# Attention times values in whole float32, two heads in one bank, in a fused attention and two-layer-stack kernel

## The chip, the cores and the metric

The kernel runs on one core of one Trainium2 chip, as one launch. The metric is the device time of that launch in microseconds, the median of several executions. The core's engines are TensorE (PE in the profile; PEld is its loading of stationary operands), VectorE (DVE), ScalarE (ACT), GpSimd (POOL) and SyncE (SP), which here only issues transfers. Each engine works through its own instructions in the order of the program and waits for others by semaphores.

## What is computed

Inputs are whole float32. Three stages follow each other: causal attention with a decay, a maximum of three projections, and a rational function between two projections.

```python
scores = q @ k.T / 8                      # (4, 8, 576, 576), head_dim 64
decay  = cum[:, :, :, None] - cum[:, :, None, :]      # cum = cumsum(log(clip(f)))
scores = where(causal, -1e9, scores + decay)
attn   = softmax(scores)                  # with 1e-9 in the denominator
x = (attn @ v)                            # -> (2304, 512)
h = maximum(maximum(x @ w1, x @ w2), x @ w3)          # d_ff 768
x2 = h @ w_out                            # (2304, 512)
g = P(x2 @ w_in) / (Q(x2 @ w_in) + 1e-6)  # d_ff 2048, P cubic, Q quadratic
out = g @ w_out2
```

## The kernel before

The eight heads of a batch are taken as four **pairs**, two heads side by side in 128 partitions or columns. The 576 queries form two **groups** `g`: queries 0 to 319 (g 0, three blocks) and 320 to 575 (g 1, two blocks). A **unit** is one head and one group of a pair. The loop over `slots` takes one unit a step: in step s the unit's scores are made and exponentiated (`scores`, L348 on), in step s+1 its probabilities are turned (`turn`, L392 on: TensorE transposes into `tp`, copies into `pt`), in step s+2 they are multiplied with the values (`attend`, L427 on). Batch 0 has eight pairs of one group each; the other three batches have twelve pairs of both groups. There are 32 products of a pair and a group in all, each for two heads.

**Two ways of a product.** TensorE multiplies either whole float32 (`F32`) or a shorter format (`F32R`). Pairs 0 to 5 (`WHOLE`) use whole float32: `turn` copies `tp` once (L418), `attend` multiplies with 64 columns of values (L437), and each head's result lies in `ot[0:64]`. The other 14 pairs (2 with g 1 alone, 12 with both groups: 26 pair-groups, 52 units) use two F32R parts. ACT copies the high part (L420), DVE subtracts the low part (L423); POOL splits the values likewise (`split_v`, L312 and L313); the stationary operand holds 64 columns of high and 64 of low values, and the product (L449) streams the high and the low probabilities through all 128 columns: 9 matmuls for g 1, 5 for g 0. The two halves of `ot` are then added (L460 on ACT, L461 on DVE), and POOL splits the sum into two F32R parts for the next stage (L464, L465).

**Beside it** the planner `fill`, called six times a step, spreads three kinds of other work over the steps: the first layer of the next stage for batches whose attention is done (`moe1_h` L489 to L496, `moe1_o` L513 to L518), the conversion of weights (`convert`, L162 to L172: `cv_w`, `cv_wo`, and from step 32 `cv_wp`), and the preparation of the next pair's keys and queries. A scheduler orders each engine's instructions from this program; it may move them across steps. For the first four pairs `exercised` puts two matmuls on a constant (L81) ahead of each new bank. The bank pool `ps_o` of the product has one buffer.

After the loop the weights of the last stage are converted (`cv_wi`), and the last stage (L736 to L796) runs on TensorE, untouched by the change.

Of the kernel before, what the change touches and what calls it, by code (L numbers as in the profile page):

```python
# [34 lines left out]
def kernel(  # L35
# [60 lines left out]
    ones = apool.tile([NR, S], F32, name="ones", tag="e4")  # L96
# [34 lines left out]
    vn = apool.tile([P, NB, 2, D], F32, name="vn")  # L131
# [7 lines left out]
    ptfs = {}  # L139
# [94 lines left out]
    class Pair:  # L234


        def __init__(self, n, b, hp, groups):
# [5 lines left out]
            self.x32, self.vs = {}, {}  # L243
# [10 lines left out]
        def load_v(self):  # L254
            b, h0 = self.b, 2 * self.hp
            if self.whole:
                self.v = apool.tile([P, NB, 2, D], F32, name=f"v_{self.n}", tag="vs", bufs=3)
                load_nat(self.v, v, b, h0, 0, self.nk)
                return
            load_nat(vn, v, b, h0, 0, self.nk)  # L260
            nc.sync.dma_start(vn[D:P, 0], v[b, h0 : h0 + 2, 0:D].rearrange("h p d -> p h d"))
# [61 lines left out]
    class Unit:  # L323


        def __init__(self, pair, h, g):
            self.pair, self.h, self.g, self.nm = pair, h, g, f"{pair.n}_{h}_{g}"
            self.e = {}

            self.alt = pair.b == 0 and h == 1  # L330

        def begin(self):
            if self.alt:
                name = f"ea_{self.nm}"
                if self.g == 0:
                    ea = [apool.tile([P, 576], F32, name=name + "2", tag="e4")]
                    ea.append(apool.tile([P, 448], F32, name=name + "1", tag="e3"))
                    self.e = {2: ea[0][:, :320], 1: ea[1][:, :192], 0: ea[1][:, 192:256]}
                else:
                    ea = apool.tile([P, 2 * GCOLS[0]], F32, name=name, tag="pt0")  # L340
                    self.e = {4: ea[:, :576], 3: ea[:, 576:1024]}
# [5 lines left out]
        def scores(self, i):  # L347
# [6 lines left out]
            if not self.alt:  # L354
                self.e[i] = apool.tile([P, keys], F32, name=f"e{i}_{self.nm}", tag=f"e{i}")
# [33 lines left out]
        def turn(self, bank):  # L389

            g = self.g
            hi = GQ[g][1]  # L392
            if self.pair.whole:
                if g not in ptfs:
                    ptfs[g] = apool.tile([P, 2, GCOLS[g]], F32, name=f"ptf{g}", tag=f"pt{g}")
                self.pt = ptfs[g][:, self.h]
            elif bank == 0:
                tag = f"pt{1 if self.alt else g}"
                self.pt = apool.tile([P, 2, GCOLS[g]], F32R, name=f"pt_{self.nm}", tag=tag)
            pt = self.pt  # L400
# [16 lines left out]
            if self.pair.whole:  # L417
                nc.scalar.activation(pt[:kr, base : base + n], tp[:kr, :n], AF.Copy)  # L418
                return
            nc.scalar.activation(pt[:kr, 0, base : base + n], tp[:kr, :n], AF.Copy)  # L420

            lo = pt[D:P, 0] if chunks[0] == 0 else pt[:, 1]
            nc.vector.tensor_tensor(  # L423
                lo[:kr, base : base + n], tp[:kr, :n], r32(pt[:kr, 0, base : base + n]), op=ALU.subtract
            )

        def attend(self):  # L427
            p, h, g = self.pair, self.h, self.g
            lo, hi = GQ[g]
# [3 lines left out]
            a, o = SIDES[h]  # L433
            if p.whole:
                for j, (c, (col, q0)) in enumerate(order):
                    kr = Q1[c] - Q0[c]
                    nc.tensor.matmul(  # L437
                        ot[0:D, q0 - lo : w], p.v[:kr, c, h], self.pt[:kr, col : col + hi - q0],
                        start=(j == 0), stop=(j == len(order) - 1),
                    )  # L440
                if h == 0:
                    xt[p.b, p.hp, g] = mpool.tile([P, 2, w], F32R, name=f"x_{self.nm}", tag=f"x{g}", bufs=(6, 8)[g])
                x = xt[p.b, p.hp, g]
                nc.scalar.activation(x[a, 0], ot[0:D, :w], AF.Copy)
                nc.vector.tensor_tensor(x[a, 1], ot[0:D, :w], r32(x[a, 0]), op=ALU.subtract)
                return
            for j, (c, (col, q0)) in enumerate(order):
                for s in range(1 if c == 0 else 2):
                    nc.tensor.matmul(  # L449
                        ot[:, q0 - lo : w],  # L450
                        p.vs[h][:, c].rearrange("p t d -> p (t d)"),
                        self.pt[:, s, col : col + hi - q0],
                        start=(j == 0 and s == 0),
# [138 lines left out]
    for p in pairs:  # L592
# [4 lines left out]
        if p.n:  # L597
            lvat.setdefault(max(0, at - LV), []).append(p)
# [264 lines left out]
```

## Time and profile before

| | us |
|---|---|
| median of 3 runs (lowest, highest) | 1027.72 (1026.54, 1028.21) |
| the profiled execution | 1026.19 |
| its span, first to last instruction | 1024.4 |
| PE, DVE, ACT, POOL busy | 977.5, 845.5, 624.6, 358.3 |

The profiled execution takes 1.8 us more than its span. A matmul's recorded time includes the way through the array, and the next starts before it ends; so what a matmul costs is read from the start of it to the start of the next, and a PE that is shown as busy may still hold gaps. In a row of the timeline the first number is the start, the second the time from the first start to the last end, both in us, and x9 counts the instructions merged. A row of groups has the source line, engine, operation, output and inputs, shape and count, then the busy time in us and the mean of one in ns, then the engine's idle time ahead of it and who ended that. A row of stretches has the stretch, its length, and for PE, PEld, DVE, ACT and POOL the busy time in us with the number of instructions, then the share of full clock that TensorE was granted, the transfers' share and their GB/s. The line of a chain gives the shares of a stretch that lines had in the chain of work that ended last.

### The profile page before, as it was taken

How to read it: one execution, taken by the hardware profiler on the slowest of the kernel's cores; microseconds unless marked ns; L12 is line 12 of the kernel's file. 1: busy time of each engine (PE TensorE's matmuls, PEld its weight loads, DVE VectorE, ACT ScalarE, POOL GpSimd, SP SyncE). 2: the span in 40 equal slices, each digit the busy share in tenths (PEclk: the TensorE clock that was granted, in tenths of full speed). 3: DMA queues.
4: the chain of work that ended last, by engine and by line, in shares of the span. 5: the costliest groups of instructions: out<-in, count | busy, mean ns of one | idle time of the engine just before them, and what ended most of it. 6: DMA issues, size and time to landing. Idle time of an engine off the chain costs nothing.

```text
span 1024.4 us, 17331 instructions
## 1 busy us (share of the span) xinstructions
PE 977.5 (95%) x5736; PEld 852.7 (83%) x5736; DVE 845.5 (83%) x1908; ACT 624.6 (61%) x1441; POOL 358.3 (35%) x606
## 2 busy tenths in 40 slices
PE   8989889998899999999999889999999999999998
PEld 5657777996888888899999788888888888899997
DVE  4779998778888988975759785998988888799997
ACT  4675656557555555554544335866666766677775
POOL 1536766666566666664636450000000000000000
PEclk9999999998899998999999999999999999999999
DMA  4664223123234434512034628501101100200000
GB/s 124 167 169 136 75 52 102 31 57 107 76 108 132 150 110 147 168 48 77 9 103 125 196 83 288 205 1 42 42 0 62 42 1 1 81 23 1 31 1 31
DMA packets 120472, 87.16 MB, mean 85 GB/s; under 512 B 69296, under 2 KB 105152, under 8 KB 120384
## 3 DMA queue, kind: packets, MB, share of 16 engines
q1 hardware_dynamic: 120384, 86.08, 27.6%
q8 instruction: 45, 0.74, 0.3%
q14 instruction: 43, 0.35, 0.1%
HBM read 63.36 MB, written 22.69 MB: 84 GB/s over the span
## 4 chain that ended last, share of the span: by engine, by line
PE 64%; DVE 20%; issue 5%; ACT 4%; POOL 3%; DMA 3%; SPq 1%; POOLq 0%; DVEq 0%; ACTq 0%
PE oo L786 6%; PE oo L787 6%; PE oo L785 6%; PE hq L736 6%; PE hq L738 6%; PE hq L737 6%; PE tp L413 4%; PE h L489 3%; PE h L490 3%; PE h L491 3%; PE o L449 2%; DVE e L371 2%; DVE pt L423 2%; DVE cv_wp L163 2%; DVE m L496 1%
## 5 line engine op out<-in xcount | busy, mean ns | idle before, releaser
L489 PE MATMUL h<-x,w1h 128*128 128x320 f32 (+1 forms) x576 | 176.1, 306 | 5.9 <-DVE m L496 3.6
L490 PE MATMUL h<-x,w1h 128*128 128x320 f32 (+1 forms) x576 | 172.2, 299 | 0.0
L491 PE MATMUL h<-x,w1l 128*128 128x320 f32 (+1 forms) x576 | 171.3, 298 | 0.0
L489 PEld LDWEIGHTS h<-x,w1h 128*128 128x128 f32 x576 | 109.6, 190 | 10.4 <-DVE m L496 5.4
L786 PE MATMUL oo<-wp,gh 128*128 128x512 f32 x288 | 112.8, 392 | 0.0
L785 PE MATMUL oo<-wp,gh 128*128 128x512 f32 x288 | 112.4, 390 | 0.0
L377 ACT ACTIVATE e<-e,st 64x64 f32<-64x64 f32 (+4 forms) x140 | 78.2, 559 | 52.8 <-DVE st L371 50.1
L490 PEld LDWEIGHTS h<-x,w1h 128*128 128x128 f32 x576 | 109.8, 191 | 0.4 <-issue 0.2
L491 PEld LDWEIGHTS h<-x,w1l 128*128 128x128 f32 x576 | 109.5, 190 | 0.1
L787 PE MATMUL oo<-wp,gl 128*128 128x512 f32 x288 | 108.8, 392 | 0.0
L745 ACT ACTIVATE s<-hq 128x512 f32<-128x512 f32 (+1 forms) x80 | 44.3, 554 | 97.2 <-PE hq L738 97.1
L387 POOL TENSOR_SCALAR e<-e,rs 64x64 f32<-64x64 f32 (+4 forms) x140 | 76.8, 560 | 62.1 <-DVE rs L383 46.4
L748 DVE SCALAR_TENSOR_TENSOR s<-s,ab,u 128x512 f32<-128x512 f32 (+1 forms) x80 | 55.9, 698 | 30.9 <-ACT u L746 30.7
L423 DVE TENSOR_TENSOR pt<-tp,pt 128x384 fp32r<-128x384 f32 (+3 forms) x132 | 69.9, 539 | 10.2 <-ACT pt L420 7.8
L371 DVE CUSTOM_DVE_ANT_0 e<-s,mask 128x320 f32<-128x320 f32 (+3 forms) x140 | 58.8, 431 | 22.7 <-PE s L367 9.0
L413 PE MATMUL tp<-ident,e 128*128 128x128 f32 (+2 forms) x420 | 70.8, 283 | 2.9 <-POOL e L387 1.4
L420 ACT ACTIVATE pt<-tp 128x384 fp32r<-128x384 f32 (+3 forms) x132 | 57.7, 473 | 24.5 <-PE tp L413 23.4
L738 PE MATMUL hq<-x,wil 128*128 128x512 f32 (+1 forms) x192 | 70.4, 366 | 0.0
L736 PE MATMUL hq<-x,wih 128*128 128x512 f32 (+1 forms) x192 | 70.4, 366 | 0.0
L737 PE MATMUL hq<-x,wih 128*128 128x512 f32 (+1 forms) x192 | 70.3, 366 | 0.0
L513 PE MATMUL x2p<-hh,wo 128*128 128x320 f32 (+1 forms) x192 | 58.5, 307 | 9.6 <-POOL hh L500 7.9
L787 PEld LDWEIGHTS oo<-wp,gl 128*128 128x128 f32 x288 | 54.1, 188 | 11.6
(145 smaller groups left out, 2718.9 us busy)
## 6 DMA issues: line engine op xcount, KB each, us to landing
raw_w<-in_moe_w_dram SPq DMA_DIRECT2D x18, 512.0 KB
raw_wp<-in_moe_w_out_dram SPq DMA_DIRECT2D x32, 256.0 KB
wpd<-wp SPq DMA_DIRECT2D x32, 256.0 KB
raw_wi<-in_moe_w_in_dram SPq DMA_DIRECT2D x32, 256.0 KB
wp<-wpd SPq DMA_DIRECT2D x10, 768.0 KB
x2d<-xo SPq DMA_DIRECT2D x16, 320.0 KB
out_dram<-ob SPq DMA_DIRECT2D x18, 256.0 KB
kn<-in_k_dram SPq DMA_DIRECT2D x32, 128.0 KB
```

The source lines that it names most:

```text
L371: nc.vector.tensor_tensor_reduce(out=e[:nr, a:z], in0=sp[:nr, : z - a], in1=mask[:nr, off + a : off + z], scale=-1.0, scalar=3.0e38 if n = ...
L413: nc.tensor.transpose(tp[:kr, dst : dst + nr], self.e[i][:nr, Q0[c] : Q1[c]], ident[:nr, :nr])
L423: nc.vector.tensor_tensor(lo[:kr, base : base + n], tp[:kr, :n], r32(pt[:kr, 0, base : base + n]), op=ALU.subtract)
L489: nc.tensor.matmul(hp_[:, :w], wh[:, j, dc], xs[dc][:, 1], start=(dc == NDC - 1), stop=False)
L490: nc.tensor.matmul(hp_[:, :w], wh[:, j, dc], xs[dc][:, 0], start=False, stop=False)
L491: nc.tensor.matmul(hp_[:, :w], wl[:, j, dc], xs[dc][:, 0], start=False, stop=(dc == 0))
L736: nc.tensor.matmul(hp_[:, :w], wih[:, dc, fs], xh, start=(dc == 0), stop=False)
L737: nc.tensor.matmul(hp_[:, :w], wih[:, dc, fs], xl, start=False, stop=False)
L738: nc.tensor.matmul(hp_[:, :w], wil[:, dc, fs], xh, start=False, stop=(dc == NDC - 1))
L785: nc.tensor.matmul(o, g[0][:, ts_], wh_, start=(fc == 0), stop=False)
L786: nc.tensor.matmul(o, g[0][:, ts_], wl_, start=False, stop=False)
L787: nc.tensor.matmul(o, g[1][:, ts_], wh_, start=False, stop=(fc == NF2 - 1))
```

## The change

Every product of probabilities and values is made in whole float32. `split_v`, the low part of `pt`, the sum of halves and the split on POOL are gone; values are loaded straight into one of three buffers `vs`. A product waits until both heads of a pair and group are turned; it is issued once for both, alternating between them, head 0 into `ot[0:64]` and head 1 into `ot[64:128]` (`SIDES`), each with a stationary operand of 64 columns. The result is copied by ACT and its rest subtracted by DVE, both on 128 partitions. Units of a pair are ordered group 0 head 0, group 0 head 1, group 1 head 0, group 1 head 1, where it was head by head. The score tiles `e` have a buffer for each head, so the borrowed tiles (`alt`) of batch 0 go.

```diff
         def load_v(self):
             b, h0 = self.b, 2 * self.hp
-            if self.whole:
-                self.v = apool.tile([P, NB, 2, D], F32, name=f"v_{self.n}", tag="vs", bufs=3)
-                load_nat(self.v, v, b, h0, 0, self.nk)
-                return
-            load_nat(vn, v, b, h0, 0, self.nk)
-            nc.sync.dma_start(vn[D:P, 0], v[b, h0 : h0 + 2, 0:D].rearrange("h p d -> p h d"))
+            self.v = apool.tile([P, NB, 2, D], F32, name=f"v_{self.n}", tag="vs", bufs=3)
+            load_nat(self.v, v, b, h0, 0, self.nk)
...
-        def split_v(self, h):
-            if self.whole:
-                return
-            nk = self.nk
-            vs = apool.tile([P, NB, 2, D], F32R, name=f"vs{h}_{self.n}", tag="vs", bufs=3)
-            pinned(nc.gpsimd.tensor_scalar(vs[:, :nk, h], vn[:, :nk, h], 1.0, 0.0, op0=ALU.mult, op1=ALU.add))
-            nc.gpsimd.tensor_tensor(vs[:, :nk, 1 - h], vn[:, :nk, h], r32(vs[:, :nk, h]), op=ALU.subtract)
-            self.vs[h] = vs
...
-            if not self.alt:
-                self.e[i] = apool.tile([P, keys], F32, name=f"e{i}_{self.nm}", tag=f"e{i}")
+            self.e[i] = apool.tile([P, keys], F32, name=f"e{i}_{self.nm}", tag=f"e{i}_{h}")
...
-            if self.pair.whole:
-                nc.scalar.activation(pt[:kr, base : base + n], tp[:kr, :n], AF.Copy)
+            nc.scalar.activation(pt[:kr, base : base + n], tp[:kr, :n], AF.Copy)
+
+        def attend(self):
+
+            p, h, g = self.pair, self.h, self.g
+            if h == 0:
                 return
-            nc.scalar.activation(pt[:kr, 0, base : base + n], tp[:kr, :n], AF.Copy)
-
-            lo = pt[D:P, 0] if chunks[0] == 0 else pt[:, 1]
-            nc.vector.tensor_tensor(
-                lo[:kr, base : base + n], tp[:kr, :n], r32(pt[:kr, 0, base : base + n]), op=ALU.subtract
-            )
...
-            if p.whole:
-                for j, (c, (col, q0)) in enumerate(order):
-                    kr = Q1[c] - Q0[c]
+            for j, (c, (col, q0)) in enumerate(order):
+                kr = Q1[c] - Q0[c]
+                for i in range(2):
                     nc.tensor.matmul(
-                        ot[0:D, q0 - lo : w], p.v[:kr, c, h], self.pt[:kr, col : col + hi - q0],
+                        ot[SIDES[i][0], q0 - lo : w], p.v[:kr, c, i], p.pt[g][:kr, i, col : col + hi - q0],
                         start=(j == 0), stop=(j == len(order) - 1),
                     )
...
-            half = apool.tile([P, 320], F32, name=f"half_{self.nm}", tag="half")[:, :w]
-            nc.scalar.activation(half[a], ot[o, :w], AF.Copy)
-            nc.vector.tensor_tensor(x32[a], ot[a, :w], half[a], op=ALU.add)
-            if h == 1:
-                x = mpool.tile([P, 2, w], F32R, name=f"x_{self.nm}", tag=f"x{g}", bufs=(6, 8)[g])
-                nc.gpsimd.tensor_scalar(x[:, 0], x32, 1.0, 0.0, op0=ALU.mult, op1=ALU.add)
-                nc.gpsimd.tensor_tensor(x[:, 1], x32, r32(x[:, 0]), op=ALU.subtract)
-                xt[p.b, p.hp, g] = x
+            x = mpool.tile([P, 2, w], F32R, name=f"x_{self.nm}", tag=f"x{g}", bufs=(6, 8)[g])
+            nc.scalar.activation(x[:, 0], ot[:, :w], AF.Copy)
+            nc.vector.tensor_tensor(x[:, 1], ot[:, :w], r32(x[:, 0]), op=ALU.subtract)
+            xt[p.b, p.hp, g] = x
...
-    slots = [Unit(p, h, g) for p in pairs for h in range(2) for g in p.groups]
+    slots = [Unit(p, h, g) for p in pairs for g in p.groups for h in range(2)]
```

On PE the product of head 1 and g 1 of pair 17 (`o`, from the turned `pt` and the split values `vs`) stands like this before, amid the second projection of the first layer (`x2p`) and the next pair's scores (`s`):

```order
L514 MATMUL x2p_0_3_6588<-hh_0_4_6262,wo_1445 128x320
L449 MATMUL o_1_1_6572<-pt_1_1_6478,vs_17_6346 128x256 x7
L449 MATMUL o_1_1_6572<-pt_1_1_6478,vs_17_6346 128x128 x2
L515 MATMUL x2p_0_3_6588<-hh_0_4_6262,wo_1445 128x320
L513 MATMUL x2p_0_3_6588<-hh_0_5_6422,wo_1542 128x320
L514 MATMUL x2p_0_3_6588<-hh_0_5_6422,wo_1542 128x320
L515 MATMUL x2p_0_3_6588<-hh_0_5_6422,wo_1542 128x320
L369 MATMUL s_0_18_0_1_6642<-k1s_1112,q1s_1175 128x448
```

One head's nine matmuls stand together, on 128 output partitions; head 0's nine stand at another place. For the same pair and group the changed program has, with the product now at L399 and `v` unsplit:

```order
L455 MATMUL x2p_0_2_6010<-hh_0_5_5907,wo_1499 128x320
L399 MATMUL o_1_1_6038<-pt_0_1_5853,v_5518 64x256
L453 MATMUL x2p_0_3_6052<-hh_0_0_5268,wo_1075 128x320
L454 MATMUL x2p_0_3_6052<-hh_0_0_5268,wo_1075 128x320
L455 MATMUL x2p_0_3_6052<-hh_0_0_5268,wo_1075 128x320
L453 MATMUL x2p_0_3_6052<-hh_0_1_5423,wo_1175 128x320
L454 MATMUL x2p_0_3_6052<-hh_0_1_5423,wo_1175 128x320
L455 MATMUL x2p_0_3_6052<-hh_0_1_5423,wo_1175 128x320
L453 MATMUL x2p_0_3_6052<-hh_0_2_5543,wo_1252 128x320
L454 MATMUL x2p_0_3_6052<-hh_0_2_5543,wo_1252 128x320
L455 MATMUL x2p_0_3_6052<-hh_0_2_5543,wo_1252 128x320
L399 MATMUL o_1_1_6038<-pt_0_1_5853,v_5518 64x256 x7
```

Both heads' products stand together, on 64 output partitions each, and the first one (head 0, keys 0 to 63) was moved ahead of nine other matmuls, alone. It stands apart in 29 of the 32 products.

On DVE, in the stretch where the scheduler works on pairs 13 and 14, the program before has the low parts of `pt` between the conversion of weights (`cv_wp`) and the masking of scores (L371, printed as ISA):

```order
L168 SCALAR_TENSOR_TENSOR cv_wp_0_4485<-raw_wp_0_4311,cv_wp_0_4485 128x256
L423 TENSOR_TENSOR pt_1_1_4425<-tp_13_1_1_4426,pt_1_1_4425 128x512
L165 SCALAR_TENSOR_TENSOR cv_wp_1_4572<-raw_wp_1_4370,cv_wp_1_4572 128x256
L371 ISA e_14_0_1_4604,st_0_1_4602<-s_0_14_0_1_4605,mask 128x448
L371 ISA st_0_1_4602 128x1
L518 TENSOR_TENSOR xo_0_2_4452<-x2p_0_2_4433,xo_0_2_4452 128x320
L371 ISA e_14_0_1_4628,st_0_1_4602<-s_0_14_0_1_4629,mask 128x320
L371 ISA st_0_1_4602 128x1
L423 TENSOR_TENSOR pt_1_1_4425<-tp_13_1_1_4456,pt_1_1_4425 128x384
L423 TENSOR_TENSOR pt_1_1_4425<-tp_13_1_1_4462,pt_1_1_4425 64x256
```

The changed program, near the end of pair 13's attention, has there (masking is now L344):

```order
L344 ISA e_14_1_0_4251,st_1_0_4248<-s_0_14_1_0_4252,mask 64x64
L344 ISA st_1_0_4248 64x1
L355 TENSOR_SCALAR rs_0_0_4121<-rs_0_0_4121 128x3
L356 RECIPROCAL rs_0_0_4121<-rs_0_0_4121 128x3
L458 TENSOR_TENSOR xo_0_3_4166<-x2p_0_3_4147,xo_0_3_4166 128x320
L161 TENSOR_SCALAR cv_wp_0_4290<-cv_wp_0_4290 128x256
L162 TENSOR_SCALAR cv_wp_0_4290<-cv_wp_0_4290 128x256
L163 SCALAR_TENSOR_TENSOR cv_wp_0_4290<-raw_wp_0_4135,cv_wp_0_4290 128x256
L166 SCALAR_TENSOR_TENSOR cv_wp_0_4290<-raw_wp_0_4135,cv_wp_0_4290 128x256
L405 TENSOR_TENSOR x_1_1_4207<-o_1_1_4196,x_1_1_4207 128x256
```

The low parts are gone; one subtraction for a pair and group (L405) stands in place of two sums (L461).

## Rows read from the trace of the kernel before

**Rows 1.** The page, part 1: busy us (share of the span) and instructions
```profile
PE 977.5 (95%) x5736; PEld 852.7 (83%) x5736; DVE 845.5 (83%) x1908; ACT 624.6 (61%) x1441; POOL 358.3 (35%) x606
```
**Rows 2.** Busy time by stretch: PE, PEld, DVE, ACT, POOL, clock, transfers
```profile
130.00:260.00 130.00, 120.46 (x864) 108.99 (x865) 105.62 (x312) 82.76 (x232) 83.61 (x163) 0.96 0.27 69
260.00:400.00 140.00, 128.94 (x901) 118.93 (x900) 126.08 (x337) 80.88 (x230) 89.71 (x156) 0.96 0.40 120
400.00:540.00 140.00, 139.23 (x1043) 134.54 (x1043) 99.23 (x287) 74.42 (x206) 80.02 (x144) 0.99 0.28 84
640.00:1024.00 384.00, 380.60 (x1742) 322.15 (x1740) 338.88 (x552) 263.83 (x470) 0.00 (x0) 1.00 0.11 38
```
**Rows 3.** The chain's shares by line: stretches 0 to 60, 130 to 260, 260 to 400, 400 to 540
```profile
by line: PE s L81 15.2%; PE s L367 13.0%; PE o L437 12.3%; PE tp L81 10.2%; PE tp L413 7.4%; SPq L228 5.3%; SPq L225 4.2%; DMA ncd<-nch 3.5%; PE o L81 3.4%; ACT cv_w L162 3.0%; PE tk L294 2.6%; PE tq L294 2.6%; DMA kf<-ncd 2.6%; ACT kf L268
...
by line: PE tp L413 11.9%; PE o L449 7.4%; PE h L489 6.9%; PE h L490 6.9%; PE h L491 6.8%; issue 6.0%; PE s L369 4.7%; PE s L370 4.1%; PE x2p L513 3.3%; PE x2p L514 3.2%; POOL e L387 3.2%; PE x2p L515 3.1%; DVE e L371 2.8%; PE tk L294 2.5%;
...
by line: issue 12.8%; DVE cv_wp L163 9.7%; DVE e L371 8.7%; DVE cv_wp L165 7.7%; DVE pt L423 7.6%; DVE cv_wp L168 5.1%; DVE m L496 4.5%; DVE k2s L272 4.2%; DVE q1s L284 3.7%; PE tp L413 3.1%; DVE cv_wp L164 2.8%; ACT e L377 2.8%; DVE x L461
...
by line: PE h L489 11.5%; PE h L490 11.2%; PE h L491 11.2%; PE tp L413 8.7%; PE o L449 7.8%; PE x2p L513 4.6%; PE x2p L515 4.6%; PE x2p L514 4.6%; PE s L369 3.2%; PE s L370 3.2%; issue 2.9%; DVE pt L423 2.9%; DVE cv_wp L163 2.2%; DVE e L371
```
**Rows 4.** Groups of the lines that go, whole span: busy us, mean ns
```profile
L423 DVE TENSOR_TENSOR pt<-tp,pt 128x384 fp32r<-128x384 f32 (+3 forms) x132 | 69.9, 539 | 10.2 <-ACT pt L420 7.8
...
L313 POOL TENSOR_TENSOR vs<-vn,vs 128x320 fp32r<-128x320 f32 x28 | 24.8, 886 | 1.1
L461 DVE TENSOR_TENSOR x<-o,half 64x256 f32<-64x256 f32 (+1 forms) x52 | 23.5, 451 | 9.8 <-ACT half L460 8.8
...
L465 POOL TENSOR_TENSOR x<-x,x 128x256 fp32r<-128x256 f32 (+1 forms) x26 | 21.1, 813 | 0.8
L460 ACT ACTIVATE half<-o 64x256 f32<-64x256 f32 (+1 forms) x52 | 21.0, 404 | 15.9 <-PE o L449 14.6 <-PE s L370 0.5
```
**Rows 5.** Groups by form: the nearest to the copies that come
```profile
L518 DVE TENSOR_TENSOR xo<-x2p,xo 128x320 fp32r<-128x320 f32 x16 | 7.7, 489 | 8.0 <-ACT xo L517 7.9
...
L517 ACT ACTIVATE xo<-x2p 128x320 fp32r<-128x320 f32 x16 | 6.7, 431 | 9.6 <-DMA x2d<-xo 5.1 <-PE x2p L515 3.1 <-PE s L369 0.9
```
**Rows 6.** Timeline: whole float32 products of one head, g 1, then g 0
```profile
95.84 2.30 PE L437 MATMUL o<-ptf,v 64*64 64x256 f32 x10
98.07 0.48 PE L367 MATMUL s<-kf,qf 66*128 66x256 f32 x1
...
96.41 1.49 PEld L437 LDWEIGHTS o<-ptf,v 128*64 128x64 f32 x8 [0.39 <-issue]
...
29.46 1.54 PE L437 MATMUL o<-ptf,v 64*64 64x320 f32 x6
30.94 0.73 PE L81 MATMUL tp<-warm 128*128 128x512 f32 x2
```
**Rows 7.** Timeline: F32R products of one head, g 1, then g 0
```profile
193.19 1.15 PE L449 MATMUL o<-pt,vs 128*128 128x256 f32 x9
194.18 0.20 PE L369 MATMUL s<-k1s,q1s 128*64 128x64 f32 x1
...
197.13 0.73 PE L449 MATMUL o<-pt,vs 128*128 128x320 f32 x5
197.70 0.51 PE L413 MATMUL tp<-ident,e 128*128 128x128 f32 x3
```
**Rows 8.** Stretches, L461 alone on DVE: two of it for a product
```profile
130.00:260.00 130.00, 8.04 (x18) 0.96 0.27 69
260.00:400.00 140.00, 7.25 (x16) 0.96 0.40 120
400.00:540.00 140.00, 8.16 (x18) 0.99 0.28 84
```
**Rows 9.** Groups by form: one conversion step, beside attention and after it
```profile
L163 DVE TENSOR_SCALAR cv_wp<-cv_wp 128x256 f32<-128x256 f32 x32 | 25.3, 800 | 1.8 <-ACT cv_wp L162 1.5
...
L163 DVE TENSOR_SCALAR cv_wi<-cv_wi 128x256 f32<-128x256 f32 x32 | 13.0, 406 | 1.3 <-ACT cv_wi L162 1.3
```

More of the change, by code (lines that the diff above doesn't have):

```diff
@@ L95 @@
     nc.sync.dma_start(fl, f.rearrange("b h s -> (b h) s"))
-    ones = apool.tile([NR, S], F32, name="ones", tag="e4")
+    ones = apool.tile([NR, S], F32, name="ones", tag="e4_0")
     nc.vector.memset(ones, 1.0)
@@ L129, in q_split @@
         return kqs[g, i]
-    vn = apool.tile([P, NB, 2, D], F32, name="vn")
     NA = GQ[0][1]
@@ L138 @@
         nc.vector.tensor_copy(qf[D : D + 2], ones[0:2, :NA])
-    ptfs = {}
     w1t, wot = {}, {}
@@ L242, in __init__ @@
             self.iq = [[(2 * n + h) % m for h in range(2)] for m in NQB]
-            self.x32, self.vs = {}, {}
+            self.pt = {}
             self.whole = n < WHOLE
@@ L328, in __init__ @@
             self.e = {}
-            self.alt = pair.b == 0 and h == 1
         def begin(self):
[L333 to L341, printed above, removed]
             self.st = apool.tile([P, 9], F32, name=f"st_{self.nm}", tag="st", bufs=3)
@@ L389, in turn @@
         def turn(self, bank):
-            g = self.g
+            g, p = self.g, self.pair
             hi = GQ[g][1]
-            if self.pair.whole:
[L394 to L400, printed above, removed]
+            if g not in p.pt:
+                p.pt[g] = apool.tile([P, 2, GCOLS[g]], F32, name=f"pt_{self.nm}", tag=f"pt{g}")
+            pt = p.pt[g][:, self.h]
             chunks = GBANK[g][bank]
@@ L416, in turn @@
                 n += hi - q0
-            if self.pair.whole:
-                nc.scalar.activation(pt[:kr, base : base + n], tp[:kr, :n], AF.Copy)
-                return
-            nc.scalar.activation(pt[:kr, 0, base : base + n], tp[:kr, :n], AF.Copy)
-            lo = pt[D:P, 0] if chunks[0] == 0 else pt[:, 1]
-            nc.vector.tensor_tensor(
-                lo[:kr, base : base + n], tp[:kr, :n], r32(pt[:kr, 0, base : base + n]), op=ALU.subtract
-            )
+            nc.scalar.activation(pt[:kr, base : base + n], tp[:kr, :n], AF.Copy)
         def attend(self):
             p, h, g = self.pair, self.h, self.g
+            if h == 0:
+                return
             lo, hi = GQ[g]
@@ L439, in attend @@
                         start=(j == 0), stop=(j == len(order) - 1),
                     )
[L441 to L453, printed above, removed]
-                        stop=(j == len(order) - 1 and s == 1),
-                    )
@@ L456, in attend @@
-            if h == 0:
-                p.x32[g] = apool.tile([P, 320], F32, name=f"x32_{self.nm}", tag="x32", bufs=2)
-            x32 = p.x32[g][:, :w]
-            half = apool.tile([P, 320], F32, name=f"half_{self.nm}", tag="half")[:, :w]
-            nc.scalar.activation(half[a], ot[o, :w], AF.Copy)
-            nc.vector.tensor_tensor(x32[a], ot[a, :w], half[a], op=ALU.add)
-            if h == 1:
-                x = mpool.tile([P, 2, w], F32R, name=f"x_{self.nm}", tag=f"x{g}", bufs=(6, 8)[g])
-                nc.gpsimd.tensor_scalar(x[:, 0], x32, 1.0, 0.0, op0=ALU.mult, op1=ALU.add)
-                nc.gpsimd.tensor_tensor(x[:, 1], x32, r32(x[:, 0]), op=ALU.subtract)
-                xt[p.b, p.hp, g] = x
+            x = mpool.tile([P, 2, w], F32R, name=f"x_{self.nm}", tag=f"x{g}", bufs=(6, 8)[g])
@@ L590 @@
     LV = 1
-    svat, lvat = {}, {}
-    for p in pairs:
-        full = len(p.groups) == 2
-        at = first[p.n]
-        for h in range(2):
-            svat.setdefault(at + h * (1 + full), []).append((p, h))
-        if p.n:
-            lvat.setdefault(max(0, at - LV), []).append(p)
+    lvat = {}
+    for p in pairs[1:]:
+        lvat.setdefault(max(0, first[p.n] - LV), []).append(p)
     for f_ in pairs[0].prepare():
@@ L641 @@
             u.normalise()
-        for p, h in svat.get(step, []):
-            p.split_v(h)
         for p in lvat.get(step, []):
```

1 line of the change is left out of this document (removed).

## Prediction

> **What bounds the kernel now.** I read the page's first part, then busy times by stretch, then the chain by stretch, and last the costs of single products in the timeline. Over the whole span PE looks like the bound, 95% busy [rows 1]; but the last stage, 384 us in which PE is busy 380.6, is untouched by the change [rows 2]. What is decided lies in the 410 us of attention from 130 to 540 us, and these are three different stretches. From 260 to 400 us DVE is busy 126.08 of 140 us, since the conversion of weights runs beside attention there, and its chain is led by DVE lines (L163 9.7%, L371 8.7%, L165 7.7%, L423 7.6%) with almost no PE [rows 2, 3]. From 400 to 540 us PE is busy 139.23 of 140 and its lines lead the chain [rows 2, 3]. From 130 to 260 us PE leads as well, with gaps. So DVE's work that goes is worth most in the middle, and PE's work that comes costs most at both ends.
>
> **What goes.** L423 takes 69.9 us of DVE, L461 23.5; on ACT L460 takes 21.0; on POOL L313 and L465 take 45.9, with two cheaper lines beside them [rows 4]. In their place come, for each of 32 products, one copy on ACT (nearest row 0.431 us, 13.8 in all) and one subtraction on DVE (0.489 us, 15.6 in all) [rows 5]. DVE is some 80 us lighter, ACT some 10, POOL over 46. SP issues 28 fewer transfers; after 60 us no line of SP stands in the lists of the chain [rows 3], so I cost that at nothing.
>
> What of it lay on the path I take from the chain. The 26 products that change their kind fall 9, 8 and 9 into the three stretches (two L461 for each) [rows 8].
> - 130 to 260 us: L423 and L461 are not among the lines of 2.5% (3.2 us) or more, so between 0 and 6.4 us together. The lines on ACT and POOL are not listed either. I take 5 for all, less 1 for the new subtractions: 4.
> - 260 to 400 us: L423 is 7.6% of 140, 10.6 us; L461 stands right behind 2.8%, so at most 3.9 us [rows 3]. That is 14.5 us on the chain. At the other end, all that DVE loses there: 8 of 26 parts of 93.4 us, 28.7, less 8 subtractions of 0.489, 24.8. With DVE busy 90% of the time [rows 2] its queue is nearly without gaps, and pieces off the chain delay it too; I take 20, nearer to the upper end.
> - 400 to 540 us: L423 is 2.9%, 4.1 us [rows 3]; with the rest 6, less 1: 5.
>
> Together 29 us. A little more: one step of the conversion takes 0.800 us on average beside attention and 0.406 us after it [rows 9]. I read the difference, 32 times 0.394 or 12.6 us, as DVE waiting for POOL; with a fifth of POOL's work gone and half of L163 on the path I count 1 us.
>
> **What comes on PE.** One head's product in F32R takes 0.99 us for g 1 (193.19 to 194.18) and 0.57 for g 0, so a pair 1.98 and 1.14 [rows 7]. In whole float32 a head takes 2.23 us for g 1 (95.84 to 98.07) and 1.48 for g 0; each matmul is recorded twice, ten records for five matmuls [rows 6]. The first of these, 64 keys in a quarter of the array, takes 0.57 us (95.84 to 96.41), the other 896 columns 1.66, or 0.47 for 256 [rows 6]: a change of the tile's shape costs some 0.1 us. Weight loading stood idle there for 0.39 us on nothing that the profile shows.
>
> The trace of before has no two matmuls in different halves of the columns, so how far they overlap is bounded from both sides: not at all, or whole. The order shows head 0's first matmul alone in 29 of 32 products, and head 1's first stands ahead of a change of shape; neither has a partner. The rest alternate. With whole overlap g 1 costs 0.67 (head 0's first with the way back to full tiles), 0.57, 1.66 for both heads' rest and about 0.2 for the half that ends later: 3.1 us against 1.98, so 1.1 more. g 0: 0.77, 0.67, 0.81 and 0.15, 2.4 against 1.14, 1.26 more. For 14 products of g 1 and 12 of g 0 that is 30.5 us. Without any overlap it is 4.6 against 1.98 and 3.15 against 1.14: 60.5 us. I take whole overlap for the alternating part, because the two read different columns of the array and write different partitions, and a half product already leaves half of the array idle in the rows of before.
>
> First the row: the change of shape at 96.41 us costs about 0.1 us [rows 6]. The Trainium skill (TensorEngine Tiling (Array Packing), Key Properties) says of it that changing the tiling mode drains TensorE, and of two tiles of one mode that they run in parallel; by the first the trace agrees, the second no row here shows. The Trainium skill (TensorE: Matmul & The Clock Gate, Part 3) gives three column tiles as 2.38 times as fast, not 3; an estimate from that page, 79% of the ideal for the alternating part, would add 9 us of PE and put the time near 1020.
>
> How much of it is on the path: L449 holds 7.4% of 130 us, 9.6 us, where 9 products take 14.3 us by [rows 7] (mean 1.59), so two thirds; from 400 to 540 us 7.8%, 10.9 us, so three quarters; in the middle less than 2.8% [rows 3]. The stretches get 10.6, 9.4 and 10.6 us more. On the path that is 7.1 and 8.1 at the ends; in the middle PE comes closer to being last as DVE leaves, so between 2.9 and 9.4, and I take 4.7. Together 20 us.
>
> **Early pairs.** Pairs 0 to 5 did whole float32 one head after the other, so they gain. For four products of g 0 2.96 becomes 2.4, of which L437's 12.3% of 60 us, 7.4 of 11.8 us, was on the path [rows 3, 6]: 1.4 us. Half of the exercise ahead of bank `o` (L81, 3.4% of 60 us, 2.0) goes: 1 us [rows 3]. The two products of g 1 fall into a stretch where L437 leads no longer; 1 us of 2.7.
>
> **Order and waits.** With units by group, a product waits for the second head, one step more, and PE gets it in a lump of 2.4 to 3.1 us where it had 0.57 to 0.99. Behind it on PE stand the next scores, which DVE (L371) and then ACT wait for; DVE's own lighter queue hides that in the middle, and at the ends it is in the shares above. The first matmul, moved ahead, needs the one bank of `ps_o`; behind it PE would stand until ACT's copy and DVE's subtraction of the product before are done. Before, the bank had twice as many uses, and no wait of PE for L461 stands among the lines of the chains [rows 3]: nothing. Score tiles of their own for each head loosen waits; I count nothing for that either.
>
> **The sum** against the profiled execution, 1026.2: minus 29, minus 1, plus 20, minus 3.4 gives 1012.8. The median of before lies 1.5 us above that execution, so **1014 us**.
>
> **Rivals.**
> *The halves do not run side by side.* Then the change does not do what its words say. PE gets 60.5 us more instead of 30.5: 20.9, 18.6 and 20.9 by stretch. At two thirds, half and three quarters to all that is 14.0, 9.3 and 15.7 to 20.9, some 42 us on the path; the early products gain nothing, only the exercise 1. 1026.2 minus 30, minus 1, plus 42: 1037, with the 1.5 us 1039. This is the side slower than before: it decides from about 31 us on the path, that is when only half of the alternating part's time is shared. Against it: 64 output columns are half an array. For it: no row shows two matmuls at once.
> *DVE's work had cover.* The middle stretch gives only half of its 14.5 us on the chain, 7, since ACT's exponentials (L377 2.8%) and 12.8% of issue time stand in the same chain [rows 3] and become last; the ends give 4 together. Minus 11, minus 4.4, plus 16 to 20: 1027 to 1031, with the 1.5 us about 1030. For it: POOL is busy 89.71 and PE 128.94 of the 140 us as well [rows 2]. Against it: DVE leads that chain by its own lines.
> *DVE was the only bound in the middle.* All 24.8 us come back, and PE's own there costs 0 to 2.9: 1004 to 1007.
>
> TensorE's clock was granted 0.96 on average in the first two stretches and 0.99 in the third [rows 2], so in some 8% of the time it was at 1.2 GHz, after stretches in which PE had waited. Fewer waits could give up to some 5 us back, more waits take as much; that widens the range only.
>
> **How the numbers follow.** The forecast, with its better variant down to 1004, gets 0.63; cover 0.20; no overlap 0.17. The range, 1000 to 1034, reaches from whole overlap with DVE's full gain and a steadier clock, over the case of cover, to a part of the case without overlap. A measurement of this kernel can tell about 0.2%, 2 us, from no change. Faster: nearly all of the first (0.60) and a third of the second: 0.68. Same: 0.07, from the seam between them. Slower: most of the second and all of the third, 0.25.
>
> **What would show it.** Side by side: in the timeline after, two records with the same start a few ns apart in each product, and nine or ten records of g 1 in 1.7 us; without, 3.3 us. DVE: some 80 us less busy, and the middle stretch shorter by 15 us or more while the last one before 540 us grows by 3. Wrong I would be if PE showed waits ahead of the moved first matmul, if the middle stretch kept its length with DVE at 70%, or if the stage after attention moved in length.

## The result and the profile after

The changed kernel takes **1014.37 us** (median of 4, 1012.68 to 1014.65), the kernel before 1027.97 (1026.54 to 1028.72) beside it: a ratio of 0.9859, 95% interval 0.9835 to 0.9883. The forecast was 1014. The number held, but by luck in part: the sum behind it counted what goes and what comes too large and the early pairs too small, and these errors cancelled.

The first row is part 1 of the page after, busy us and share of the span of 1012.8 us, then the group of the product; they answer to [rows 1].

```profile
PE 984.6 (97%) x5780; PEld 831.2 (82%) x5780; DVE 750.6 (74%) x1744; ACT 613.5 (61%) x1409; POOL 286.7 (28%) x498
...
L399 PE MATMUL o<-pt,v 128*64 128x256 f32 (+3 forms) x512 | 83.0, 371 | 0.3 <-ACT pt L385 0.3
```

From this the shortest ledger follows. PE's idle time, span less busy, was 1024.4 - 977.5 = 46.9 us and is 1012.8 - 984.6 = 28.2: 18.7 us less. PE's busy time rose by 7.1. Net 11.6, the whole difference of the two spans. The product took 55.0 + 21.6 = 76.6 us of PE before (the groups of L449 and L437) and takes 83.0. That is recorded time, in which a matmul's way through the array lies over the next matmul. Added up over the traces from each matmul's start to the start of the next ("by starts" from here on; to its own end where PE then idles), it is 46.8 + 20.8 = 67.6 us before and 78.5 after.

Busy time by stretch after (PE, PEld, DVE, ACT, POOL, clock, DMA share, GB/s), to be laid beside [rows 2]; attention now ends some 12 to 14 us earlier, so the third stretch ends at 528.

```profile
130.00:260.00 130.00, 126.83 (x897) 106.38 (x897) 77.72 (x272) 81.19 (x231) 61.84 (x126) 0.97 0.25 66
260.00:400.00 140.00, 138.68 (x996) 118.59 (x995) 97.04 (x306) 84.78 (x238) 70.61 (x132) 1.00 0.46 140
400.00:528.00 128.00, 128.00 (x924) 111.90 (x924) 60.55 (x200) 60.92 (x169) 48.25 (x93) 1.00 0.22 65
```

DVE is at 97 of 140 us in the middle instead of 126, and PE at 138.7 instead of 128.9. PE's idle time in the three stretches was 9.5 + 11.1 + 0.8 = 21.4 us and is 3.2 + 1.3 + 0 = 4.5: nearly all of the 18.7 us come from here. The chain by line, middle stretch of after, has gone from DVE's lines to PE's [rows 3]:

```profile
by line: PE o L399 12.3%; PE h L429 10.7%; PE h L430 10.2%; PE h L431 10.2%; PE tp L381 8.2%; DMA raw_wp<-in_moe_w_out_dram 5.7%; issue 4.7%; PE s L342 3.5%; PE s L343 3.3%; PE x2p L453 2.7%; DVE cv_wp L163 2.5%; DVE q1s L278 2.3%; PE x2p L
```

The timeline of PE after (start, us, line, tile, count) shows one pair's product for g 1, then one for g 0:

```profile
258.40 0.64 PE L399 MATMUL o<-pt,v 64*64 64x256 f32 x2
...
262.18 2.31 PE L399 MATMUL o<-pt,v 64*64 64x256 f32 x18
264.41 1.06 PE L381 MATMUL tp<-ident,e 128*128 128x128 f32 x6
...
269.65 1.56 PE L399 MATMUL o<-pt,v 64*64 64x320 f32 x12
271.14 0.41 PE L430 MATMUL h<-x,w1h 128*128 128x320 f32 x1
```

Head 0's first matmul stands alone at 258.40. The other 18 records, ten of head 1 and eight of head 0, take 262.18 to 264.41, 2.23 us: what ten records of one head took before [rows 6]. The g 0 product is one of the three whose first matmul was not moved: twelve records of two heads in 1.49 us, where six of one head took 1.48 [rows 6]. In the trace the records of a pair start 6 to 7 ns apart (303.790 and 303.797, 304.057 and 304.063 us).

One step of the weights' conversion, by form, beside attention [rows 9]:

```profile
L161 DVE TENSOR_SCALAR cv_wp<-cv_wp 128x256 f32<-128x256 f32 x32 | 12.1, 384 | 13.7 <-ACT cv_wp L160 13.5
```

It took 800 ns before and takes 384. DVE's last step on `cv_wp` ends at 422.3 us instead of 449.2.

### The profile page after: what moved, and what is told of

Read it like the earlier page. It is cut to its first block, busy times and chain, and to the rows that moved or that the text cites. A ratio compares the mean times of both kernels' runs of the same rounds, so it can differ in the third digit from the quotient of the medians.

```text
span 1012.8 us, 16900 instructions
## 1 busy us (share of the span) xinstructions
PE 984.6 (97%) x5780; PEld 831.2 (82%) x5780; DVE 750.6 (74%) x1744; ACT 613.5 (61%) x1409; POOL 286.7 (28%) x498
## 4 chain that ended last, share of the span: by engine, by line
PE 77%; DVE 14%; issue 3%; DMA 3%; ACT 2%; POOL 1%; SPq 0%; DVEq 0%; POOLq 0%; ACTq 0%
PE oo L719 7%; PE oo L720 7%; PE oo L718 6%; PE o L399 6%; PE hq L669 6%; PE hq L671 6%; PE hq L670 6%; PE tp L381 5%; PE h L429 5%; PE h L430 4%; PE h L431 4%; PE s L342 2%; PE x2p L453 2%; PE x2p L455 2%; PE x2p L454 2%
## 5 line engine op out<-in xcount | busy, mean ns | idle before, releaser
L360 POOL TENSOR_SCALAR e<-e,rs 64x64 f32<-64x64 f32 (+4 forms) x160 | 88.6, 565 | 114.5 <-DVE rs L356 87.9
L350 ACT ACTIVATE e<-e,st 64x64 f32<-64x64 f32 (+4 forms) x160 | 89.3, 558 | 51.7 <-DVE st L344 48.9
L344 DVE CUSTOM_DVE_ANT_0 e<-s,mask 128x320 f32<-128x320 f32 (+3 forms) x160 | 68.1, 432 | 57.6 <-PE s L343 37.3
L385 ACT ACTIVATE pt<-tp 128x384 f32<-128x384 f32 (+3 forms) x160 | 69.8, 471 | 31.6 <-PE tp L381 28.7
L399 PE MATMUL o<-pt,v 128*64 128x256 f32 (+3 forms) x512 | 83.0, 371 | 0.3 <-ACT pt L385 0.3
L381 PE MATMUL tp<-ident,e 128*128 128x128 f32 (+2 forms) x480 | 81.4, 278 | 0.6 <-POOL e L360 0.5
L381 PEld LDWEIGHTS tp<-ident,e 128*128 128x128 f32 (+2 forms) x480 | 54.3, 132 | 13.6 <-issue 7.0
```

The source lines that it names most:

```text
L350: nc.scalar.activation(e[:nr], e[:nr], AF.Exp, bias=m, scale=-1.0, accum_out=l)
L381: nc.tensor.transpose(tp[:kr, dst : dst + nr], self.e[i][:nr, Q0[c] : Q1[c]], ident[:nr, :nr])
L399: nc.tensor.matmul(ot[SIDES[i][0], q0 - lo : w], p.v[:kr, c, i], p.pt[g][:kr, i, col : col + hi - q0], start=(j == 0), stop=(j == len(orde ...
```

## The experiments

The runs were made on four occasions, each with the kernel before beside them; its median there was 1034.5 (e1, e2, e3, c0), 1029.3 (e4, e5, e7), 1030.8 (e6, e8, e10) and 1030.0 us (e11, e12). Its single executions lay between 1024.0 us, at a mean granted clock of 0.99, and 1036.2, at 0.972. Taken by the ratios to before in place of the medians, the differences below move by up to 5 us (e4 over c0 is then 5 and not 1, c0 over after 3 and not 7), so a few us between different occasions mean little. PE's idle time is span less busy of the profiled execution.

| kernel | median us | PE busy | PE idle | product on PE |
|---|---|---|---|---|
| after | 1014.4 | 984.6 | 28.2 | 83.0 |
| e1 head by head | 1055.6 | 1029.3 | 24.8 | 126.8 |
| e2 late head first | 998.7 | 968.6 | 30.2 | 63.5 |
| e3 old order of units | 1012.9 | 984.4 | 26.4 | 83.3 |
| e7 e2 and e3 | 1000.0 | 970.0 | 30.5 | 64.0 |
| c0 two value buffers | 1021.3 | 994.0 | 28.2 | 86.8 |
| e4 c0, DVE's work | 1022.1 | 990.7 | 29.8 | 86.3 |
| e5 c0, POOL's work | 1027.1 | 988.8 | 34.8 | 85.0 |
| e6 after, DVE's work in between | 1019.8 | 988.6 | 29.7 | 86.4 |
| e10 c0, both | 1037.1 | 999.1 | 36.5 | 86.7 |
| e12 after, both in between | 1031.4 | 994.5 | 33.5 | 88.9 |
| e11 e3, tiles shared after batch 0 | 1023.7 | 989.5 | 29.0 | 81.7 |
| e8 e3, tiles shared | 1037.5 | 1001.3 | 35.6 | 87.0 |

**Sharing the array: e1.** The two loops of the product are swapped, so that one head's matmuls follow the other's.

```
-            for j, (c, (col, q0)) in enumerate(order):
-                kr = Q1[c] - Q0[c]
-                for i in range(2):
+            for i in range(2):
+                for j, (c, (col, q0)) in enumerate(order):
+                    kr = Q1[c] - Q0[c]
```

> The changed kernel with one edit: all matmuls of head 0 are issued ahead of those of head 1, so that matmuls of the two halves of the array seldom stand next to each other. Nothing else differs. Theory (the halves run side by side, and that is worth its time): a product of g 1 costs 4.5 us instead of 2.8 and one of g 0 about 3.0 instead of 2.2, some 40 us more of PE over 32 products, of which two thirds lie on the path: 1036 to 1045 us, above the kernel before. Rival (sharing is worth little, since PE had room): 1012 to 1018 us.

Measured: 1055.63 us, ratio to before 1.0242 (1.0181 to 1.0302), above the range of the theory, since nearly all that PE got more, and not two thirds, came into the time. The timeline of PE in e1, ten records of one head:

```profile
153.73 2.30 PE L399 MATMUL o<-pt,v 64*64 64x256 f32 x10
155.96 0.41 PE L453 MATMUL x2p<-hh,wo 128*128 128x320 f32 x1
```

Ten records take the 2.23 us that eighteen of both heads took. The product takes 126.8 us instead of 83.0; of these 43.8, 41 are in the time. The two halves do run side by side, and without that the change would have made the kernel slower.

**The lone first matmul: e2.** Head 1, whose probabilities are ready last, comes first in the product, so nothing of it can be moved ahead.

```
-                for i in range(2):
+                for i in (1, 0):
```

> The changed kernel with one edit: in each pair of matmuls head 1, whose probabilities come a step later, is issued ahead of head 0, so that the first matmul can't be moved ahead alone and has its partner behind it. Theory (the lone first matmul of head 0 costs 0.57 us and two changes of the tile's shape): 32 times 0.7 us, 22 us less of PE, of which two thirds lie on the path: 997 to 1003 us. Rival (the lone matmul stood in gaps of PE and cost nothing): 1012 to 1017 us.

Measured: 998.70 us (998.04 to 1000.60), ratio to before 0.9680 (0.9628 to 0.9732): the fastest kernel of this study, 15.7 us under after. The timeline of PE in e2:

```profile
255.99 2.31 PE L399 MATMUL o<-pt,v 64*64 64x256 f32 x20
258.23 1.06 PE L381 MATMUL tp<-ident,e 128*128 128x128 f32 x6
...
263.48 1.56 PE L399 MATMUL o<-pt,v 64*64 64x320 f32 x12
264.96 0.41 PE L429 MATMUL h<-x,w1h 128*128 128x320 f32 x1
```

All twenty records of g 1 take 2.24 us. The product takes 63.5 us on PE, 19.5 less than after (17.6 by starts), and less than the 76.6 of before. For 29 products that is 0.61 to 0.67 us each: about the slot of a matmul that has lost its partner (0.58, from 258.40 to 258.98 in after) and a change of tile shape.

**The order of the units: e3 and e7.** The units stand head by head again, in e3 with the rest as in after, in e7 together with e2.

```
-    slots = [Unit(p, h, g) for p in pairs for g in p.groups for h in range(2)]
+    slots = [Unit(p, h, g) for p in pairs for h in range(2) for g in p.groups]
```

> The changed kernel with the units in the old order: head 0 with both groups, then head 1 with both. Products are still made for two heads at once, later by one step for g 0. Theory (the gain comes from DVE's work that went, the order counts for little): 1010 to 1019 us. Rival (the order of the units, with its shorter wait of a group for its second head, gave the gain): 1022 us or more.

> The kernel with the late head first, and the units in the old order, head by head. Theory (order counts for nothing, the pairing of all matmuls for 14 to 16 us): 995 to 1001 us. Rival (with the product a step later and none of it moved ahead, PE waits for it): 1004 us or more.

Measured: 1012.94 and 999.98 us, each within 1.5 us of its partner. The order by group brings and costs nothing that can be told from the noise.

**A control: c0.** Two value buffers instead of three, as room for the tiles of the next runs; two early tiles move to other buffers.

```
-            self.v = apool.tile([P, NB, 2, D], F32, name=f"v_{self.n}", tag="vs", bufs=3)
+            self.v = apool.tile([P, NB, 2, D], F32, name=f"v_{self.n}", tag="vs", bufs=2)
```

> A control for later runs: the changed kernel with two buffers instead of three for the values, and the two tiles of the start that shared them placed elsewhere. Both theories: 1012 to 1017 us, as the changed kernel.

Measured: 1021.29 us (1019.23 to 1023.99), 7 more than after; a miss. PE idles just as long (28.2); it is busy 9.4 longer, 3.8 of them in the product. Its profiled execution had a mean granted clock of 0.985 where after had 0.989; by these two shares of the spans, some 4 of the 9.4 us are an estimate for the clock. Whether the buffer itself or the shifted order on PE does the rest was not tried. An edit that was meant to do nothing moves this kernel by several us, and terms of that size can't be told apart here.

**DVE's work alone: e4 and e6.** In e4 (on c0) DVE again subtracts once for each turned bank, 132 steps, into a tile that nobody reads. In e6 (on after) DVE's step stands between the turn and the product, so that PE waits for it; it takes the larger of two equal numbers.

```
+                low = apool.tile([P, 512], F32, name=f"low{bank}_{self.nm}", tag="low")
+                nc.vector.tensor_tensor(low[:kr, :n], tp[:kr, :n], pt[:kr, base : base + n], op=ALU.subtract)
...
+                both = pt[:kr, base : base + n]
+                nc.vector.tensor_tensor(both, tp[:kr, :n], both, op=ALU.max)
```

> The control with two value buffers, and DVE makes the low parts of the turned probabilities again for the 14 pairs that had them before, into a tile that nobody reads: 132 subtractions, some 70 us of DVE, and nothing else. Theory (DVE's work was on the path in the middle stretch, 260 to 400 us, where the conversion of weights runs): 15 to 24 us over the control, 1036 to 1045 us, most of it in that stretch, with DVE busy 85% or more there. Rival (DVE's work had cover, and the gain came from POOL or the order): within 5 us of the control, 1018 to 1026 us.

> The changed kernel, and for the 14 pairs that had low parts before, DVE takes the larger of the turned probabilities in PSUM and their copy, which are the same numbers, and writes them over the copy: 132 steps of the cost of a low part, some 70 us of DVE, and now PE's product waits for them, as it waited for the low parts. Theory 1 (what the low parts cost was PE's wait for them, not DVE's time): 15 to 24 us over the changed kernel, 1029 to 1038 us. Theory 2 (neither the time nor the wait was on the path): 1012 to 1020 us.

Measured: e4 1022.08 us, 1 over its control; e6 1019.75, 5 over after. My theory fell in both, and the other expectation held. The middle stretch of e4 by busy time, and its chain by line:

```profile
260.00:400.00 140.00, 136.80 (x963) 115.45 (x962) 112.66 (x348) 84.80 (x243) 69.27 (x132) 0.99 0.45 132
...
by line: PE o L402 16.9%; PE h L432 13.0%; PE h L433 12.6%; PE h L434 12.6%; PE tp L381 10.7%; PE s L342 4.6%; PE s L343 4.2%; PE x2p L456 3.3%; PE x2p L457 2.7%; PE x2p L458 2.7%; PE tk L288 2.5%; DMA raw_wp<-in_moe_w_out_dram 2.3%; PE tq
```

DVE has 112.66 us of work, 15.6 more than in after and only 13 less than before, and no line of DVE is among those listed, of 2.3% or more. At 80% DVE hardly holds PE up.

**POOL's work alone, and both: e5, e10, e12.** e5 (on c0) gives POOL the splitting of values (four blocks of five) and of results again, into a tile that nobody reads. e10 is e5 with e6's step. e12 (on after, with its three buffers) has e6's step and POOL's work in place, on the values and on the result itself, times one and plus zero, so that PE waits for all of it. The edit of e12:

```
+            part = self.v[:, 1 : self.nk, h]
+            pinned(nc.gpsimd.tensor_scalar(part, part, 1.0, 0.0, op0=ALU.mult, op1=ALU.add))
+            zeros = mask[:, : (self.nk - 1) * D].rearrange("p (c d) -> p c d", d=D)
+            nc.gpsimd.tensor_tensor(part, part, zeros, op=ALU.add)
...
+                nc.gpsimd.tensor_scalar(x[:, 0], r32(x[:, 0]), 1.0, 0.0, op0=ALU.mult, op1=ALU.add)
+                nc.gpsimd.tensor_tensor(x[:, 1], r32(x[:, 1]), mask[:, :w], op=ALU.add)
```

> The control with two value buffers, and POOL does work again like that which the change removed, into a tile that nobody reads: 28 splits of values (four of five blocks each) and 26 splits of the result, some 60 us of POOL. Theory (POOL was off the path; it only delays DVE's conversion steps by 0.2 to 0.4 us each): 0 to 5 us over the control, 1020 to 1026 us, with the first conversion step back at 0.6 us or more. Rival (POOL's work gave a good part of the gain): 8 us or more over the control, 1029 us or more.

> The control with two value buffers (1021 us), with both kinds of work back: DVE's steps between copy and product, and POOL's splits into a tile that nobody reads. All that the change took away is there again, but for the sum of halves. Theory 1 (DVE and POOL each had room, but not both, since they hold each other up): 20 to 33 us over the control, 1041 to 1054 us. Theory 2 (each costs what it costs alone, 1 and 6 us): 1024 to 1032 us.

> The changed kernel with three value buffers, and the work of both engines back in place, on the tiles that PE reads: DVE's step on the turned probabilities, POOL's two on each head's values (four of five blocks) and on each result. PE waits for all of it, as it did before. Theory 1 (DVE's and POOL's work together, with their waits, are the greater part of what the change gave): 16 to 26 us over the changed kernel, 1030 to 1040 us, most of it between 260 and 400 us. Theory 2 (they have cover, and score tiles are the greater part): 1019 to 1026 us.

Measured: e5 1027.07 us, 6 over c0, between its two forecasts; e10 1037.05, 16 over c0, again between the two; e12 1031.42 (ratio to before 1.0023, 1.0000 to 1.0046), 17 over after, as its first theory said. So with all the work of both engines back the changed kernel is about as slow as the kernel before. DVE's step in e10 is that of e6, which costs 5 alone; with POOL's 6 that makes 11, where both cost 16. That the two together cost more than their sum is likely, but 5 us are no more than occasions can differ by. One place where they meet is the conversion. Two of its steps by form (busy us, mean ns), in c0, in e10 and in e12:

```profile
L161 DVE TENSOR_SCALAR cv_wp<-cv_wp 128x256 f32<-128x256 f32 x32 | 12.2, 388 | 9.8 <-ACT cv_wp L160 9.7
L163 DVE SCALAR_TENSOR_TENSOR cv_wp<-raw_wp,cv_wp 128x256 int32<-128x256 int32 x32 | 14.6, 463 | 0.5
```

```profile
L161 DVE TENSOR_SCALAR cv_wp<-cv_wp 128x256 f32<-128x256 f32 x32 | 19.8, 623 | 6.8 <-ACT cv_wp L160 6.7
L163 DVE SCALAR_TENSOR_TENSOR cv_wp<-raw_wp,cv_wp 128x256 int32<-128x256 int32 x32 | 18.6, 585 | 0.3
```

```profile
L161 DVE TENSOR_SCALAR cv_wp<-cv_wp 128x256 f32<-128x256 f32 x32 | 12.0, 380 | 9.4 <-ACT cv_wp L160 9.3
L163 DVE SCALAR_TENSOR_TENSOR cv_wp<-raw_wp,cv_wp 128x256 int32<-128x256 int32 x32 | 21.9, 690 | 0.4
```

The same 256 columns take 380 or 623 ns in one step, 463 or 690 in the other; which of them suffers differs between e10 and e12, where POOL's work has another place (and the values three buffers instead of two). All four DVE steps of `cv_wp` together took 71.7 us before and take 57.1 in after, 57.2 in c0, 57.6 in e6, 63.9 in e5, 69.8 in e10 and 64.9 in e12: nothing with DVE's step alone, +6.7 with POOL's work, and with both +12.6 in e10 and +7.8 in e12. The Trainium skill (SBUF — State Buffer, Who interferes with whom) says that DVE and GpSimd share a pair of ports and that the one that comes second stands still, for a DVE operation with two inputs in SBUF and for some with one. The longer steps beside POOL's work agree in part (L161 stayed at 380 ns in e12); that these steps use that pair no run here shows.

In e10 DVE is back in the chain of the middle stretch, by line:

```profile
by line: PE o L410 10.2%; PE h L444 7.0%; PE h L445 6.2%; PE h L446 6.1%; DVE cv_wp L161 6.0%; issue 5.7%; DVE cv_wp L163 5.4%; PE tp L389 4.9%; DVE e L352 4.6%; DMA raw_wp<-in_moe_w_out_dram 4.3%; PE s L350 3.9%; DVE pt L396 3.5%; PE s L35
```

It is the picture of before in a weaker form [rows 3]: conversion, masking (L352) and the turned probabilities (L396) share it.

The conversion is not the whole of it. By the ends of the results, the 16th of the 32 products is done at 275.5 us in e12 and at 265.4 in after, the 24th at 410.7 and at 392.7. So 10 us are lost up to the 16th, though DVE's first step on `cv_wp` starts only at 251.8, and 8 more up to the 24th. The expectation that most of the loss would lie between 260 and 400 us failed, and what holds the earlier stretch up was not taken apart.

**Score tiles: e8 and e11.** On e3, both heads take turns in one score tile again, in e8 everywhere, in e11 only behind batch 0. (In before, head 1 of batch 0 had borrowed tiles, so e11 is the nearer to it, and e8 is a state that neither kernel has.)

```
-            self.e[i] = apool.tile([P, keys], F32, name=f"e{i}_{self.nm}", tag=f"e{i}_{h}")
+            self.e[i] = apool.tile([P, keys], F32, name=f"e{i}_{self.nm}", tag=f"e{i}_{h if p.b == 0 else 0}")
```

> The changed kernel with the units in the old order and one set of score tiles for both heads, as before the change; products and copies as in the changed kernel. Theory 1 (the gain comes from DVE's low parts and their wait): within 4 us of the run with the old order, 1009 to 1017 us. Theory 2 (tiles of their own for each head let scores of one head be made while the other's are still read, and that gave a good part): 1021 us or more.

> The run with the old order, and score tiles of their own for each head in batch 0 alone; the three later batches share one set, as they did before the change. Theory 1 (separate tiles give several us in the later batches too, by the trace of the run with shared tiles some 7): 1017 to 1024 us. Theory 2 (what shared tiles cost lay in batch 0, where the kernel before borrowed tiles instead): 1010 to 1016 us.

Measured: e8 1037.47 us, 24.5 over e3; e11 1023.65 (ratio 0.9945, 0.9925 to 0.9966), 10.7 over e3 (7.6 between the two profiled executions). Both lie where the theory that separate tiles give a good part had put them. Each head's own score tile in the later batches is worth about 11 us, about two thirds of what DVE's and POOL's work gives back. Most of e8's loss lies in batch 0: its sixth product is done at 135.8 us instead of 118.3. In the rows, the stretch from 130 to 260 us in e11, and then in e3:

```profile
130.00:260.00 130.00, 122.18 (x852) 99.61 (x850) 71.92 (x256) 77.36 (x222) 57.90 (x120) 0.96 0.24 62
```

```profile
130.00:260.00 130.00, 126.55 (x886) 103.75 (x884) 74.33 (x268) 80.73 (x230) 60.52 (x124) 0.95 0.24 63
```

With a shared tile PE is busy 4.4 us less and gets 34 matmuls fewer done in the same 130 us. By the code head 1's masked scores can't be written before head 0's have been turned; that this wait alone makes the 10.7 us is not shown. Part of it runs through the clock: with the same 5780 matmul records PE is busy 16.9 us longer in e8 than in e3 and 5.1 longer in e11, at a mean granted clock of 0.970 and 0.983 where e3 has 0.986. From the clock and the spans alone I estimate 17 and 3 us. So waits can cost more than PE's idle time shows; that they brought the slow spells about is not shown.

## Why the prediction was right, and where it was not

**What comes on PE: the mechanism right, the size wrong.** Whole overlap was the right choice (e1, and 2.23 us for 18 records; expected were 3.1 us for g 1, and 0.58 + 2.23 = 2.8 came). But "so a pair 1.98 and 1.14" was taken from two of the quickest instances, 0.99 and 0.57 us. Over the trace the median by starts was 1.08 us for g 1 and 0.63 for g 0, and in spells with TensorE at 1.2 GHz single products took up to 1.95 and 1.15 (the mean granted clock is 0.66 to 0.84 from 240 to 270 us of before, a mixture of the two levels). So the 26 products took 46.8 us by starts, where 14 and 12 times my figures make 41.4. After, the same 26 take 64.3 by starts where my figures make 72.2. PE's product grew by 17.5 us and not by 30.5 (by recorded time from 55.0 to 67.9, by 12.9), and the 20 us on the path were 2 to 7 too many even if all of it is on the path. In all it grew by 10.9, since the early pairs fell from 20.8 to 14.3 by starts (21.6 to 15.1 recorded).

**"At two thirds, half and three quarters".** In the changed kernel PE's work is worth more than that: 41 of 43.8 us in e1, 15.7 of 17.6 to 19.5 in e2. What was counted from before's chain changed with the change, since DVE no longer stood ahead of PE.

**What goes: the step that failed is "I take 20, nearer to the upper end".** The middle stretch of before had only 140 - 128.94 = 11.1 us in which PE idled, the three together 21.4 [rows 2]. A lighter DVE can't give back more than PE's idle time, unless PE's own work gets shorter; 29 us were more than all of it. PE's own work can get shorter by the clock: at 0.96, 0.96 and 0.99 granted [rows 2], I estimate that the three stretches lost 12 us to it, of which after still loses 4 (0.97, 1.00, 1.00); my sum left that out and let it widen the range. Both bounds stood in the rows I used. After, 16.9 of the 21.4 are gone. With the early pairs at 6.7 and PE's product at 12.9 to 17.5, all that goes, score tiles and clock with it, comes to 20 to 24 us, as what is needed to reach the measured 13.6; I counted 30. And it was not DVE's own work that mattered: alone it costs 1 (e4) to 5 us (e6), POOL's alone 6 (e5), both 16 to 17 (e10, e12). The step that I read as DVE waiting for POOL and priced at **1 us** is part of the mechanism: 25.3 us became 12.1, and all four steps of `cv_wp` gave 14.6. The rival that DVE's work had cover was half right: nearly true for DVE alone, not for DVE and POOL together.

**"Score tiles of their own for each head loosen waits; I count nothing".** This failed: about 11 us (e11). The order of the units, also counted at nothing, was nothing (e3, e7).

**The first matmul, moved ahead,** was priced at 0.67 to 0.77 us a product, for 29 products 19.4 to 22.3 us of PE; e2 shows 19.5 by recorded time and 17.6 by starts. That price was about right and was also the largest thing still to be had. No wait of PE for the one bank of `ps_o` shows in the row of L399 (0.3 us in all, for ACT's `pt`).

**Early pairs** came out at -6.7 us by pair 5 (125.1 to 118.3), where -3.4 was counted: their product lost 6.5 us, the exercise ahead of `o` 2.8.

**By progress** (ends of the same pairs' results in both traces) after gains 17 us between 272 and 416 us of before's clock, where the sum had 16, and loses 9 between 416 and 534, where it had 3; the stage behind attention moved by 1. That the middle agrees is no proof of its 20: between the same two results PE has 386 matmul records of the first layer (`h`) instead of 440, with 43 more of them in the stretch before and 11 more in the one behind, and its idle time there fell by only 8.6 us, from 9.8 to 1.2. The signs named ahead of time were there: two records some ns apart, DVE 95 us less busy instead of 80, the middle shorter by 15 or more. None of them told the sizes of the two terms apart.

**What stays open.** The single prices don't add up to the result: 17 for DVE's and POOL's work, 11 for the score tiles and about 7 early make 35, and less the 12.9 to 17.5 us of PE they would leave 18 to 22, where 13.6 were measured. Each was taken with the others in place, and they fill the same idle time. Why c0 is 7 us longer, how much of e8, e10, e11 and e12 is the clock's, and how much of e10 is standing still at a port and how much is waiting in DVE's queue, was not separated.

## What to carry to other kernels

What a lighter engine can give back is bounded by the idle time of the engine that will bound next, and by what that one's own work loses to waits and to a lower clock; lay these side by side for each stretch before adding up lines of the chain. Take the cost of an operation from all its instances, start to start, not from the quickest in the timeline, on both sides of the change. In a product of two halves let the operand that is ready last come first: a matmul that a scheduler may move ahead loses its partner, and here that was worth more than the change itself.

## What the runs showed of the hardware

Two tiles of 64 columns in whole float32 share the array wholly: 20 records in 2.24 us (e2), where ten of one head take 2.23 (e1), with starts 6 to 7 ns apart. The first DVE step of the conversion, 256 columns, took 363 (e4) to 800 ns (before) on average, and POOL's total does not set it: with 349.7 us of POOL in e12 one step took 380 ns on average and another 690, with 346.0 in e10 they took 623 and 585. The spells at 1.2 GHz moved as well: in slices of 10 us the kernel before had a mean granted clock of 0.66, 0.84 and 0.81 from 240 to 270 us, after a slice in which PE was busy 8.46 of 10, and 0.82 to 0.84 from 290 to 300 and from 390 to 410. The changed kernel had 0.82 and 0.84 from 70 to 90 us, where PE was busy 5.98 of the first 10, and 0.85 from 240 to 250 (8.56 of 10). Over the span the means are 0.987 and 0.989.
